# Whole-tile stores and more crossbar transposes in a fused attention and maxout kernel

## The chip, the cores and the metric

One core of one Trainium2 chip. The metric is the device time of one execution, in microseconds (us). Executions of one kernel mostly agree within 0.3%; "fast" and "slow" below are the states that the runs were sorted into, and only fast runs are compared. A profile is one execution taken by the hardware profiler; its span is some 2 us shorter than the time.

Names used in profile lines: PE is TensorE (matmul), PEld its weight loads, DVE VectorE, ACT ScalarE, POOL GpSimd, SP SyncE, which here only issues transfers. L299 is a line of the kernel that was profiled, so line numbers shift between kernels.

## The reference

```python
# attention over pooled keys: B, H, S, D = 8, 8, 576, 64; pool = 8
k_p = k.reshape(B, H, S // 8, 8, D).mean(axis=3)
v_p = v.reshape(B, H, S // 8, 8, D).mean(axis=3)
attn = softmax(q @ k_p.T / sqrt(D))          # 576 x 72 for each batch and head
x = (attn @ v_p).transpose(0, 2, 1, 3).reshape(4608, 512)
# feed-forward with a maximum of three: 512 -> 768 -> 512
h = maximum(maximum(x @ w1, x @ w2), x @ w3)
out = h @ w_out                              # 4608 x 512, float32
```

## The kernel before

The feed-forward runs in nine blocks of 512 tokens. A block is 72 matmuls of 512 columns (hidden) and 24 (project). The attention of the next batch is slipped in between: after each group of matmuls, a "slot", a plan may call some steps. `k` turns the pooled keys, `s0` to `s7` are scores and exponentials by head, `v0` to `v4` the five 128-token chunks of values, `x0` to `x4` their transposes, `T` the transpose of q by the DMA crossbar. TensorE takes all of these in the order of the program, so a step whose input is late stops the feed-forward too (in e4 below, scores whose keys were late stopped it for 1.35 us in each of five blocks).

```python
def turn_x(b, c0, keep, xn, tag, evac=nc.scalar.copy):
    if b > 1:                                 # batches 2 to 7: by the crossbar
        nc.sync.dma_start_transpose(out=xT[:, :, g0 + keep:g0 + 128], in_=...)
        return
    ...                                       # batches 0 and 1: 4 TensorE transposes, one copy

def turn_k(b):
    pkt = keys(b, TR)                         # 6 TensorE transposes into PSUM
    for par in range(2):
        fill_kz(b, par, 0, H, pkt,
                nc.scalar.copy if b == 1 else nc.vector.tensor_copy)
...
# project: one tile is 128 tokens = two row groups (g) of 64 rows, 9 rows apart in HBM
for u in range(2):
    b, g = divmod(2 * m + u, NG)
    dst = out[S * b:S * b + S, :].rearrange("(r g) c -> r g c", g=NG)
    (nc.scalar if last and u else nc.sync).dma_start(
        out=dst[:, GS[g], c], in_=osb[64 * u:64 * u + 64, c])
...
def pool_work(n, mm):                         # called after slot 0 of block n
    if n + 2 < B:
        after([load_k(n + 2)], mm)            # GpSimd's loads for two batches on
        load_q(n + 2)
        load_v(n + 2)
```

The softmax here doesn't subtract the row's maximum and nothing guards it: scores larger than these inputs give would overflow.

## Time and profile before

| | before |
|---|---|
| time, median of the runs beside the changed kernel | 242.82 us |
| span of the profiled execution | 241.0 us |
| TensorE busy | 230.9 us, 96% |
| last matmul ends / span ends | 236.5 / 241.0 us |
| granted TensorE clock, mean | 0.998 |
| a 128 KB store, issue to landing | 2.4 us |

The table is read from the top: TensorE is the bound, and from 50 us on its matmuls start one after another at the pace that their width sets. The prediction below shows the lines.

### The profile page before, as it was taken

To read this page: it belongs to the slowest core of one execution; us is meant where nothing else is said; L and a number is where in the kernel's file an instruction comes from. 1 tells how busy PE (TensorE), PEld (TensorE's weight loads), DVE (VectorE), ACT (ScalarE), POOL (GpSimd) and SP (SyncE) were. 2 spreads that over 40 slices of the span, in tenths; PEclk is the share of its full clock that TensorE was granted. 3 is DMA by queue.
4 is the path that set the end of the run, shared out by engine and by line. 5 is a ranking of instruction groups with operands and counts; after the bars stand their busy time and mean duration, and the time that the engine had idled before them with its cause. 6 is when DMAs were issued, how large, how long until landed. Compare 5 with 4: busy or idle time off the path is not lost.

```text
span 241.0 us, 4221 instructions
## 1 busy us (share of the span) xinstructions
PE 230.9 (96%) x1609; PEld 122.7 (51%) x1609; DVE 131.7 (55%) x239; ACT 100.1 (42%) x173; POOL 123.7 (51%) x91
## 2 busy tenths in 40 slices
PE   7698999999999999999999999999999999999992
PEld 3376555575554555455545554555455544444441
DVE  6856754665583558354836483648364834504530
ACT  2373247546513651365235523552355232142121
POOL 8864276989997479638880979286500000000000
PEclk9999999999999999999999999999999999999999
DMA  7999999999948995699769987997640253043006
GB/s 135 188 198 206 196 202 208 169 166 241 184 97 153 222 166 120 128 194 197 131 125 156 227 176 133 193 192 135 133 93 0 69 123 85 3 108 66 0 20 154
DMA packets 51939, 34.29 MB, mean 142 GB/s; under 512 B 32144, under 2 KB 46480, under 8 KB 51920
## 3 DMA queue, kind: packets, MB, share of 16 engines
q0 software_dynamic: 17088, 17.11, 45.5%
q1 hardware_dynamic: 34672, 16.79, 34.3%
q8 instruction: 12, 0.20, 0.3%
q10 hardware_dynamic: 160, 0.13, 0.2%
q14 instruction: 7, 0.06, 0.1%
HBM read 34.60 MB, written 9.44 MB: 183 GB/s over the span
## 4 chain that ended last, share of the span: by engine, by line
PE 89%; DVE 5%; ACT 2%; DMA 2%; issue 1%; DVEq 0%
PE pw L295 55%; PE po L331 19%; PE psc L203 6%; PE pav L238 4%; DMA kt<-in_k_dram 2%; PE pxt L229 1%; DVE kf L362 1%; ACT et L208 1%; DVE t L304 1%; PE pkt L174 1%; PE pvp L156 1%; DVE xn L246 1%; PE pqt L167 1%; DVE kp L366 1%; DVE kf L364 1%
## 5 line engine op out<-in xcount | busy, mean ns | idle before, releaser
L295 PE MATMUL pw<-xT,mw 128*128 128x512 f16 (+2 forms) x696 | 155.6, 364 | 0.8 <-ACT xT L233 0.7
L295 PEld LDWEIGHTS <-mw 128*128 128x128 f16 x696 | 61.8, 98 | 56.2 <-issue 1.0
L304 DVE TENSOR_TENSOR t<-t,pw 128x512 f16<-128x512 f16 (+2 forms) x58 | 37.8, 651 | 71.0 <-PE pw L295 43.7
L301 ACT CAST t<-pw 128x512 f16<-128x512 f32 (+2 forms) x58 | 32.3, 556 | 56.1 <-PE pw L295 54.8
L331 PE MATMUL po<-mwo,hT 128*128 128x512 f16 (+1 forms) x222 | 50.7, 373 | 0.0
L208 ACT ACTIVATE et<-psc 72x576 f16<-72x576 f32 (+2 forms) x62 | 40.7, 662 | 20.9 <-PE psc L203 20.7
L307 DVE TENSOR_TENSOR hT<-t,pw 128x512 f16<-128x512 f16 (+2 forms) x58 | 37.7, 650 | 9.0 <-PE pw L295 5.3
L336 ACT COPY osb<-po 128x512 f32<-128x512 f32 (+1 forms) x36 | 20.9, 580 | 47.7 <-PE po L331 43.7
L135 POOL TENSOR_TENSOR half<-vt 72x2048 f32<-72x2048 f16 x7 | 28.4, 4060 | 10.0 <-DMA vt<-in_v_dram 9.9
L331 PEld LDWEIGHTS <-hT 128*128 128x128 f16 x222 | 20.3, 97 | 21.3 <-DVE hT L307 2.4
L135 POOL TENSOR_TENSOR half<-kt 96x1536 f32<-96x1536 f16 x6 | 18.5, 3085 | 23.4 <-DMA kt<-in_k_dram 23.3
L246 DVE TENSOR_TENSOR xn<-pav,rcp 128x512 f16<-128x512 f32 x39 | 27.0, 691 | 1.5 <-DVE rcp L244 0.2
L136 POOL TENSOR_TENSOR half<-half 72x1024 f32<-72x1024 f32 (+1 forms) x13 | 27.2, 2096 | 1.0
L203 PE MATMUL psc<-qT,kz 128*128 128x64 bf16 (+3 forms) x192 | 25.9, 246 | 0.4 <-DVE kz L179 0.3
L203 PEld LDWEIGHTS <-kz 128*128 128x128 bf16 x192 | 17.8, 98 | 15.7 <-DVE kz L179 1.5
L238 PEld LDWEIGHTS <-et 72*128 72x128 f16 x312 | 15.2, 98 | 7.6
L238 PE MATMUL pav<-vp,et 72*128 72x65 f16 x312 | 16.5, 194 | 0.0
L244 DVE RECIPROCAL rcp<-pav 128x8 f32<-128x8 f32 x39 | 7.9, 204 | 9.4 <-PE pav L238 9.3
L139 POOL TENSOR_TENSOR kp<-half 96x384 bf16<-96x384 f32 x12 | 11.7, 993 | 0.5
L179 DVE COPY kz<-pkt 64x576 bf16<-64x576 bf16 (+1 forms) x14 | 9.9, 711 | 2.9 <-PE pkt L174 2.7
L79 POOL DMA_DIRECT2D vt<-in_v_dram x10 | 8.0, 804 | 2.9 <-DMA qb<-in_q_dram 2.2
L139 POOL TENSOR_TENSOR vp<-half 72x512 f16<-72x512 f32 x7 | 8.9, 1268 | 0.5
(48 smaller groups left out, 79.1 us busy)
## 6 DMA issues: line engine op xcount, KB each, us to landing
out_dram<-osb SPq DMA_DIRECT2D x70, 128.0 KB, 2.4
kt<-in_k_dram POOLq DMA_DIRECT2D x7, 576.0 KB, 7.4
qb<-in_q_dram POOLq DMA_DIRECT2D x7, 576.0 KB, 12.2
vt<-in_v_dram POOLq DMA_DIRECT2D x7, 576.0 KB, 15.0
mw<-in_moe_w_dram POOLq DMA_DIRECT2D x9, 256.0 KB, 9.3
mwo<-in_moe_w_out_dram POOLq DMA_DIRECT2D x1, 768.0 KB, 18.1
qb<-in_q_dram POOLq DMA_DIRECT2D x2, 288.0 KB, 7.0
xT<-xn SPq DMA_TRANSPOSE x30, 2.4
```

The costliest lines, as they stand in the source:

```text
L135: e.tensor_tensor(out=f, in0=t[:, :, 0:4, :], in1=t[:, :, 4:8, :], op=ALU.add)
L136: e.tensor_tensor(out=f[:, :, 0:2, :], in0=f[:, :, 0:2, :], in1=f[:, :, 2:4, :], op=ALU.add)
L203: nc.tensor.matmul(out, kz_all[b % 2][:, f % 2, h, :], qTs[b][:, n + i0:n + i1, 64 * (h % 2):64 * (h % 2) + 64], start=True, stop=True)
L208: nc.scalar.activation(out=out, in_=in_, func=FT.Exp, scale=1.0 / 64.0)
L238: nc.tensor.matmul(pav[:, h // 4, 65 * (h % 4):65 * (h % 4) + 65], ets[b][:, h, c0:c0 + 128], vp_all[:, b, h, :], start=True, stop=True)
L246: nc.vector.tensor_tensor(out=xn, in0=pv[:, :, :, 0:D], in1=rcp.to_broadcast([128, 2, 4, D]), op=ALU.mult)
L295: mm = nc.tensor.matmul(pw, w_sb[wi][:, kc, bass.ts(jc, 128)], xT[:, kc, col], start=(kc == 0), stop=(kc == KCH - 1))
L301: nc.scalar.copy(out=t, in_=pw)
L304: nc.vector.tensor_tensor(out=t1, in0=t, in1=pw, op=ALU.max)
L307: nc.vector.tensor_tensor(out=hT[:, jc, c0:c1], in0=t, in1=pw, op=ALU.max)
L331: nc.tensor.matmul(po, hT[:, jc, bass.ts(mm, 128)], wo_sb[:, jc, c], start=(jc == 0), stop=(jc == JCH - 1))
L336: nc.scalar.copy(out=osb[:, c], in_=po)
```

## The change

Its intent: take transposes off TensorE (keys of batches 3 to 7, x of batch 1), shorten SyncE's queue by storing a tile with one transfer instead of two, and give the new crossbar transfers time by finer groups in blocks 0 and 1 and a later attention of batch 2.

```diff
     def turn_k(b):
-        pkt = keys(b, TR)
+        pkt = keys(b, TR) if b < 3 else kTs[b]
         for par in range(2):
             fill_kz(b, par, 0, H, pkt,
-                    nc.scalar.copy if b == 1 else nc.vector.tensor_copy)
+                    nc.vector.tensor_copy if b == 2 else nc.scalar.copy)
@@ turn_x
-        if b > 1:
+        if b > 0:
@@ do
+            elif name[0] == "Z":
+                kTs[b] = sb2.tile([128, 6, 96], BF16, name="kT", tag="kT")
+                nc.sync.dma_start_transpose(
+                    out=kTs[b], in_=kps[b].rearrange("p i a d -> p (i a d)"))
@@ hidden: half groups
-            parts = [..., (1, 2, 0, 256), (0, 2, 256, NB), (2, JCH, 0, NB)]
+            parts = [..., (1, 3, 0, 256), (0, 3, 256, NB), (3, JCH, 0, NB)]
         elif n == 1:
-            parts = [(0, 1, 0, 256), (0, 1, 256, NB), (1, JCH, 0, NB)]
+            parts = [(0, 2, 0, 256), (0, 2, 256, NB), (2, JCH, 0, NB)]
@@ project: stores
+                e = nc.scalar if last and c.start == 0 else nc.sync
+                b, g = divmod(2 * m, NG)
+                dst = out[S * b:S * b + S, :].rearrange("(r g) c -> g r c", g=NG)
+                if g < NG - 1 and GS[g] < GS[g + 1]:
+                    step = GS[g + 1] - GS[g]
+                    e.dma_start(out=dst[GS[g]:GS[g + 1] + 1:step, :, c],
+                                in_=osb[:, c])
+                    continue
                 for u in range(2):
                     ...                       # else two stores, as before
@@ plans: block 0 with its steps moved to 34 slots (cut); q of batch 2 ("T") after
@@ batch 1's x, at slot 0 of block 1; the others:
-        b, i = n + 1, 3 * (n == 1)
-        got = {0: [], 3: [], 3 + i: [(b, "k")]}
+        b, i = n + 1, 8 * (n == 1)
+        got = {2 + i: [(b, "k")]}
         got.update({5 + i + h: [(b, f"s{h}")] for h in range(H)})
-        got.update({15 + i + c: [(b, f"v{c} x{c}")] for c in range(5)})
+        got.update({14 + i + c: [(b, f"v{c} x{c}")] for c in range(5)})
+        got[17 + i].append((b + 1, "Z"))
```

A tile whose two row groups lie in one batch and ascend is stored whole: 27 of 36 in one transfer, and the last tile by column halves.

## The prediction

> **What bounds the kernel now.** I read the page's busy table first, then its chain of work that ended last, then that chain in order of time, then the timeline of TensorE and of the two queues that issue transfers (SyncE's and GpSimd's), and last the transfers by issue with their time to landing. The page:
>
> ```profile
> PE 230.9 (96%) x1609; PEld 122.7 (51%) x1609; DVE 131.7 (55%) x239; ACT 100.1 (42%) x173; POOL 123.7 (51%) x91
> ...
> PE 89%; DVE 5%; ACT 2%; DMA 2%; issue 1%; DVEq 0%
> ```
>
> TensorE is busy 96% and carries 89% of the chain. Busy alone proves little, because matmuls overlap; the chain in order of time (start, us, matmuls) settles it:
>
> ```profile
> 195.07 15.54 PE pw L295 x72
> 210.61 5.18 PE po L331 x24
> ```
>
> A block without attention is 96 matmuls of 512 columns in 20.72 us, 0.216 us each with no gap. From the trace's matmul starts I summed what each start-to-start step has beyond the usual one for its width: 9.5 us in all, of which 5.7 before 20 us, 2.0 in 20 to 30, 0.8 in 30 to 50, and under 1.1 in the whole rest. The seven blocks after the first therefore run at TensorE's own pace: only fewer or narrower matmuls can help there. Waits can be won only in block 0 (17 to 48.7 us), and block 1 begins at 48.7, block 2 at 73.4. Block 0 waits like this:
>
> ```profile
> 22.69 1.03 PE L295 MATMUL pw<-xT,mw 128*128 128x256 f16 x8 [0.67 <-ACT xT L233]
> ```
>
> The last part is the transfers around the start of block 1 (SyncE's queue, then GpSimd's, then landings of those in 49.8 to 53.8 us):
>
> ```profile
> 45.21 4.59 SPq L270 DMA_TRANSPOSE qT<-qb  x1
> 49.85 4.43 SPq L340 DMA_DIRECT2D out_dram<-osb  x6
> ```
>
> ```profile
> 46.62 1.95 POOL L139 TENSOR_TENSOR kp<-half 96x384 bf16<-96x384 f32 x2
> 49.59 0.57 POOL L72 DMA_DIRECT2D kt<-in_k_dram  x1 [1.02 <-PE pxt L229]
> 50.15 0.78 POOL L86 DMA_DIRECT2D qb<-in_q_dram  x1
> 50.93 0.85 POOL L79 DMA_DIRECT2D vt<-in_v_dram  x1
> ```
>
> ```profile
> out_dram<-osb SPq DMA_DIRECT2D x6, 128.0 KB, 7.4
> kt<-in_k_dram POOLq DMA_DIRECT2D x1, 576.0 KB, 6.7
> qb<-in_q_dram POOLq DMA_DIRECT2D x1, 576.0 KB, 11.3
> vt<-in_v_dram POOLq DMA_DIRECT2D x1, 576.0 KB, 14.3
> qT<-qb SPq DMA_TRANSPOSE x1, 6.6
> ```
>
> The reader is to see that batch 2's q transpose is issued at 45.2, ahead of the k, q and v loads of batch 3 at 49.6, and lands 6.6 us later, at 51.8; the six stores issued just after those loads took 7.4 us each, against a median of 2.4 over the kernel.
>
> **What the Trainium skill says.** "Perfetto Trace Analysis", Identifying the Most-Contended Engine: matmul busy share is a poor measure because matmuls are pipelined; the trace agrees (a 512-column matmul is listed at 379 ns but starts come every 216), so I count start-to-start time. "DMA: Bandwidth & Descriptors", Queues, rings and completion order: each DMA engine takes turns between queues packet by packet. The trace agrees: in 112 to 113 us, a q transpose beside a v load, 125 transpose packets went beside 150 load packets, and after the load's end 897 to 1030 per us went. The same page, Rules for kernel authors, prefers one 128-partition transfer to two of half the partitions; no run here shows it yet. "TensorE: Matmul & The Clock Gate", Part 1: an idle window of about 3.4 us halves the array's clock, and a busy one restores it. The trace agrees at its end: the granted clock falls to 0.5 some 3 us after the last matmul.
>
> **The change part by part.**
>
> Keys by the crossbar, batches 3 to 7: removes 5 x 6 transposes of 96 columns. Six take 0.42 us with the last one's 0.205 pipeline time, so (0.42 - 0.205)/5 = 0.043 us a step; 30 x 0.042 (the median of starts) = 1.26 us off the path. The evictions (two of 0.64 us a batch) move from VectorE to ScalarE, both about half idle, so nothing. The transfer comes eight or so slots ahead of its use, so it is hidden.
>
> Batch 1's x by the crossbar: 20 transposes of 128 columns at 0.056 us = 1.12 us off the path, and five ScalarE copies gone.
>
> Six half groups in blocks 0 and 1: 12 matmuls of 512 become 24 of 256 in each; 24 x 0.109 - 12 x 0.216 = 0.02 us each. Nothing by itself, but it gives 1.3 us more work on the first 256 columns, while x2 and x3 are being turned. Walking the new slots by hand with the old durations: the waits around x2, x3 and x4 (0.04, 0.32, 0.84 and 0.46 us) nearly vanish (0.2 left); the wait for the key sum (0.31) grows to 0.5 because the slots between are half as long, one of 0.45 appears between the key pooling and the key transposes, and the q turns keep 0.5 of 0.39; the score waits (0.08 and 0.24) shrink to 0.13. So 2.7 becomes about 1.8, 0.9 us better. Block 1 could begin at 48.7 - 0.9 - 12 x 0.056 (its other eight x transposes lay inside block 1) = 47.1 us.
>
> Whole-tile stores: most pairs of 0.54 + 0.59 us on SyncE's queue become one, I assume about 0.6. TensorE does not wait for them, but SyncE's queue gets shorter, and the tail (last matmul start 236.5, end 241.0) has one store fewer behind the last copy: 0.4 us.
>
> Sum without new waits: 1.26 + 1.12 + 0.9 + 0.4 = 3.7; 242.86 - 3.7 = 239.2 us.
>
> **What the change puts in its place.** The order of the changed kernel shows SyncE's queue at the end of block 0 as x0, store, x1, store, x2, two stores, x3, store, x4, then batch 2's q transpose, which block 0 used to issue much earlier. x0's values are made after the last hidden group, at about 42.5 us. An x transpose takes SyncE 1.31 us from issue to issue, a store 0.6: x1 at 44.5, x2 at 46.4, x3 at 49.0, q at 52.2. TensorE's first block 1 matmul waits for x0 and x1, its seventh slot for x2 and x3, and the first score of batch 2 for q.
>
> x1 shares the engines with batch 2's v load, which runs to about 48 (stores issued at 43.9 and 44.5 took 5.6 and 5.2 us). So x1 lands at about 49.6, and block 1 begins 2.5 us late. The k load of batch 3 waits for the end of slot 0 and for GpSimd (free at 48.6), so it is issued at about 50, again ahead of the q transpose. That transpose then waits for k (6.7 us), and shares packet by packet with q and v: those loads have some 1090 packets, at 150 a us 7.3 us, so till about 64; of the transpose's 2304 packets 110 to 190 a us go meanwhile, and the rest takes 1.3 us more. Landing at about 66. Without waits the first score would stand at 47.1 + 12 x 0.436 + 2 x 0.863 + 0.25 = 54.3. So TensorE waits 66 - 54.3 = 11.7 us in block 1, the 2.5 at its start included; and a wait so long halves the clock for some 3.4 us after it, 1.7 us more. Sum: 239.2 + 11.7 + 1.7 = 252.6 us.
>
> **The rivals.**
>
> First, no collision: the later attention (first score at slot 13 in place of 8) and the half groups are just what one would do to give x and q their time, which speaks for somebody having measured it. Then 239 to 240. Against it: all five later q transposes that overlapped a v load landed only 2 us or more after it.
>
> Second, a partial one: q gets its turn as soon as k is through, at about 56, and runs nearly alone: landing 58.5, a wait of 4.2 in all and perhaps no clock loss: 243.5. Against it are the 125 packets a us beside 150.
>
> Third, the collision above: 249 to 253, the lower end if x1 comes early and the loads with it.
>
> A fourth, that a new engine bounds (ScalarE with the key evictions), I rule out: it is busy 42%, and gets 10 x 0.64 us more and five copies less. Stores are off the path whatever they cost.
>
> **Range and chances.** I give the collision 0.58, the partial one 0.15, none 0.27. Only the collision is over 2% slower (over 247.7); no case reaches 2% faster (238.0) unless my block 0 walk is too dark, 0.04. The middle of this is about 249.0 us, range 239.3 to 253.5.
>
> **What would show it.** Right: in block 1 a long TensorE idle before the first scores of batch 2, put down to the q transpose, with a time to landing of over 10 us; a shorter one before the block's first matmul, put down to the x transpose; the granted clock down around 65 us; later blocks 0.25 us shorter each. Wrong: that transpose landing under 7 us, or the k load issued after it; then the time is near 239. A wait before x2 or x3 (slot 6 of block 1) would show that x3 fell behind the k load too.

## The result, and the profile after

The changed kernel took 351.5 us in the median (350.15 to 353.32, four runs), the kernel before 242.82. The ratio is 1.447 (95% interval 1.438 to 1.456). Here and below a ratio is the mean time of one kernel's fast runs over that of the other's of the same rounds, so it isn't quite the ratio of the medians quoted. The prediction was 249.0, with a range to 253.5: right in direction, and far too small.

The page of the changed kernel, its busy row, the slices of granted clock, and the chain that ended last:

```profile
PE 246.7 (71%) x1583; PEld 128.0 (37%) x1583; DVE 123.3 (35%) x232; ACT 110.2 (32%) x181; POOL 123.5 (35%) x91
PEclk9899995686998558999978995799658999999955
PE 59%; DMA 18%; SPq 10%; issue 2%; DVE 2%; ACT 2%; POOL 0%; DVEq 0%; POOLq 0%
```

Read against the lines before: TensorE's share of the chain fell from 89% to 59%, and transfers (DMA 18%) and SyncE's queue (SPq 10%) stand in the chain. TensorE now idles, and its clock is down in many slices. Whom TensorE waits for, in the view of waits (us in total, times, longest):

```profile
PE pw L299 <- DMA xT<-xn: 23.5, 4, 10.4
PE psc L203 <- ACT kz L179: 20.6, 2, 19.9
PE pw L299 <- DMA qT<-qb: 14.0, 1, 14.0
PE pw L299 <- issue: 10.7, 1, 10.7
PE psc L203 <- DMA qT<-qb: 6.1, 1, 6.1
```

Three of the five are waits for crossbar transfers. The copy kz waited in its turn (28.2 us, by the groups of instructions) for the keys' crossbar transfer, and the wait put down to "issue" ends, in the chain in order of time, behind an x transpose (from 213.83 us, 2.54 long). The chain in order of time shows how long single transfers took, where 2.3 to 8 us were usual before:

```profile
55.01 5.14 DMA xT<-xn
60.15 21.72 DMA qT<-qb
...
102.92 23.21 DMA kT<-kp
```

The prediction had the q transpose at about 14 us. The plain loads suffered too. From the transfers by issue, before and then after (KB each, median us to landing; the page of the changed kernel gives no landing time for its stores):

```profile
out_dram<-osb SPq DMA_DIRECT2D x70, 128.0 KB, 2.4
kt<-in_k_dram POOLq DMA_DIRECT2D x7, 576.0 KB, 7.4
```

```profile
out_dram<-osb SPq DMA_DIRECT2D x27, 256.0 KB
kt<-in_k_dram POOLq DMA_DIRECT2D x7, 576.0 KB, 15.1
```

A k load takes twice as long, though nothing about it was changed, and HBM traffic is the same 34.6 MB read and 9.4 written. The last matmuls, where no transpose and no load is left, show the stores alone. The end of the chain before and after:

```profile
231.33 5.21 PE po L331 x30
```

```profile
322.44 5.21 PE po L335 x30
```

Before, the span ends at 241.0, 4.5 us after the end of the last matmul (236.5); after, at 349.3, 21.7 us after it (327.6). Twenty-two microseconds of nothing but stores: what do the DMA engines do then? The stretch 330 to 340 us of the changed kernel (columns: stretch, length, five engines, granted clock, DMA share, GB/s):

```profile
330.00:340.00 10.00, 0.00 (x0) 0.00 (x0) 0.00 (x0) 0.00 (x0) 0.00 (x0) 0.60 0.13 50
```

The share of the 16 engines that is busy is 0.13, that is 2.1 of 16, at 50 GB/s. The trace's 2 KB packets say the same: 84 ns each, 25 in a microsecond, so two at a time. The Trainium skill has the rule, in "DMA: Bandwidth & Descriptors", Why a DMA increments its semaphore by 16 and not by 1: the number of engines is the largest up to 16 that divides the slowest dimension (of size other than 1) of both sides' patterns. The source's is 128 partitions, the destination's 2, so 2. Its Rules for kernel authors warn of just this ("Use all 16 engines"). At 50 GB/s a 256 KB store takes over 5 us (an estimate). How that holds up other transfers shows between 56.5 and 58.5 us, when an x transpose issued at 55.01 had not landed (it did at 60.15):

```profile
DMA packets 50, 0.10 MB, mean 51 GB/s; under 512 B 0, under 2 KB 0, under 8 KB 50
```

All 50 packets that start in these two microseconds are of 2 KB, the stores' own. None of the transpose's, which are smaller, starts.

The loss can be booked from the matmul starts. After 46 us, steps that are over 0.25 us longer than their width asks for sum to 77.8 us (before: none); the smaller excesses, nearly all of them the 427 instead of 216 ns of a 512-column matmul at half clock, to 15.7 us (before 1.0). The tail is 17.2 us longer. That is 77.8 + 14.7 + 17.2 = 109.7, less 2.4 for the transposes removed: 107.3 of the spans' difference of 108.3 us.

### The profile page after: what moved, and what is told of

It reads as the page before. It is cut to its first block, busy times and chain, and to the rows that moved or that the text cites. A ratio compares the mean times of both kernels' runs of the same rounds, so it can differ in the third digit from the quotient of the medians.

```text
span 349.3 us, 4173 instructions
## 1 busy us (share of the span) xinstructions
PE 246.7 (71%) x1583; PEld 128.0 (37%) x1583; DVE 123.3 (35%) x232; ACT 110.2 (32%) x181; POOL 123.5 (35%) x91
## 4 chain that ended last, share of the span: by engine, by line
PE 59%; DMA 18%; SPq 10%; issue 2%; DVE 2%; ACT 2%; POOL 0%; DVEq 0%; POOLq 0%
PE pw L299 36%; PE po L335 13%; DMA kT<-kp 7%; DMA qT<-qb 6%; SPq L270 6%; PE psc L203 5%; SPq L223 3%; DMA xT<-xn 3%; PE pav L238 3%; DMA qb<-in_q_dram 2%; ACT kz L179 1%; PE pqt L167 1%; PE pvp L156 1%; PE wm L363 0%; POOL kt L72 0%
## 5 line engine op out<-in xcount | busy, mean ns | idle before, releaser
L299 PE MATMUL pw<-xT,mw 128*128 128x512 f16 (+2 forms) x720 | 169.4, 381 | 49.0 <-DMA xT<-xn 23.5
L299 PEld LDWEIGHTS <-mw 128*128 128x128 f16 x720 | 67.9, 103 | 112.8 <-issue 31.5
L203 PE MATMUL psc<-qT,kz 128*128 128x64 bf16 (+3 forms) x192 | 28.1, 259 | 27.0 <-ACT kz L179 20.6
L340 ACT COPY osb<-po 128x512 f32<-128x512 f32 (+1 forms) x36 | 20.9, 580 | 56.5 <-PE po L335 44.6
L203 PEld LDWEIGHTS <-kz 128*128 128x128 bf16 x192 | 18.6, 102 | 45.2 <-ACT kz L179 22.1
L135 POOL TENSOR_TENSOR half<-vt 72x2048 f32<-72x2048 f16 x7 | 28.4, 4054 | 17.3 <-DMA vt<-in_v_dram 17.2
L179 ACT COPY kz<-kT 64x576 bf16<-64x576 bf16 x10 | 11.7, 1166 | 28.3 <-DMA kT<-kp 28.2
L72 POOL DMA_DIRECT2D kt<-in_k_dram x9 | 5.1, 565 | 31.0 <-PE pw L299 29.4
L139 POOL TENSOR_TENSOR kp<-half 96x384 bf16<-96x384 f32 x12 | 11.7, 992 | 0.5
## 6 DMA issues: line engine op xcount, KB each, us to landing
kt<-in_k_dram POOLq DMA_DIRECT2D x7, 576.0 KB, 15.1
```

The source lines that it names most:

```text
L135: e.tensor_tensor(out=f, in0=t[:, :, 0:4, :], in1=t[:, :, 4:8, :], op=ALU.add)
L203: nc.tensor.matmul(out, kz_all[b % 2][:, f % 2, h, :], qTs[b][:, n + i0:n + i1, 64 * (h % 2):64 * (h % 2) + 64], start=True, stop=True)
L299: mm = nc.tensor.matmul(pw, w_sb[wi][:, kc, bass.ts(jc, 128)], xT[:, kc, col], start=(kc == 0), stop=(kc == KCH - 1))
```

## The experiments

My theory A: the pattern of the whole-tile stores. Rival B: the crossbar collisions that I had predicted, only worse. Rival C: a large store is slow in itself. Rival D: the key transposes come late for the scores. Every kernel computes the whole result, and all twelve runs were correct.

| run | what | time, us (range) | before beside it |
|---|---|---|---|
| e1_split | changed, stores as before | 269.3 fast; 273.9 to 274.7 slow | 242.88 |
| e2_merge_only | before, whole-tile stores | 314.91 (313.03 to 315.3) | 242.88 |
| e3_interleaved | changed, stores of 64 x 2 rows | 264.73 (263.94 to 264.85) | 242.88 |
| e4_keys_only | before, keys by crossbar | 248.44 (248.06 to 250.35) | 242.88 |
| e5_keys_dve | e4, VectorE fills | 241.75 (241.53 to 242.63) | 242.79 |
| e6_keys_early | e4, one slot earlier | 241.82 (241.6 to 244.22) | 242.79 |
| e7_loads_later | e3, loads of batch 3 later | 248.84 (248.18 to 250.24) | 242.79 |
| e8_stores_interleaved_on_before | before, stores of 64 x 2 rows | 242.51 (242.37 to 243.0) | 242.79 |
| e9_combined | the parts that paid | 240.46 (239.98 to 242.31) | 243.11 |
| e10_x4_too | e9 and one x transpose | 240.15 (239.91 to 241.85) | 243.11 |
| e11_halves_2x32 | before, two stores of 2 x 32 rows | 371.55 (370.29 to 372.24) | 242.87 |
| e12_halves_4x16 | before, two stores of 4 x 16 rows | 304.29 (303.78 to 304.9) | 242.87 |

### e1_split and e2_merge_only: the stores undone, and the stores alone

```diff
 # e1, on the changed kernel; e2 is the reverse, on the kernel before
-                e = nc.scalar if last and c.start == 0 else nc.sync
-                ...                           # one whole-tile store where it fits
                 for u in range(2):
                     b, g = divmod(2 * m + u, NG)
                     dst = out[S * b:S * b + S, :].rearrange("(r g) c -> r g c", g=NG)
                     (nc.scalar if last and u else nc.sync).dma_start(
                         out=dst[:, GS[g], c], in_=osb[64 * u:64 * u + 64, c])
```

> The changed kernel with its stores as they were before: two of 64 rows for each tile in place of one whole-tile store; all else of the change kept. Theory A (the whole-tile stores, whose destination pattern is 2 x 64 rows, move on 2 of the 16 DMA engines only, and everything behind them waits): the time falls from 351.5 to 239 to 255 us, and no transfer of SyncE's queue takes over 15 us. Rival B (the crossbar transposes collide with the loads, as predicted blind): A's part is small, and it stays over 300 us. If A holds, what is left over 239 is the blind prediction's collision of batch 2's q transpose: 249 to 253 if that was right.

> The kernel before with nothing changed but its stores: whole tiles in one transfer, as in the changed kernel. Theory A: over 280 us, with waits before blocks' first matmuls put down to x transposes and q transposes. Rival B: 242 to 243 us, since no crossbar transfer is added.

e2: 314.91 us, ratio 1.294 (1.290 to 1.298), where it adds no crossbar transfer at all. Rival B can't do that. Its longest waits are for the x transposes that the kernel before already had and that never held it up (2.7 us more are for a q transpose):

```profile
PE pw L295 <- DMA xT<-xn: 40.4, 5, 12.7
```

Booked from the matmul starts like the changed kernel, e2's 72 us are some 45 of waits, 10 of lower clock and 17 of tail.

e1: one run was fast, at 269.3; the others and the profile were slow, so I take from it only that some 80 us went with the stores' pattern, and that 269 is above the 255 I had allowed. Something else was left over; e3, all of whose runs were fast, shows it better.

### e3_interleaved: the same stores, another order of rows

The maximum that writes a hidden tile puts the rows of the two groups side by side (partition 2r + u instead of 64u + r), so a store walks 64 x 2 rows instead of 2 x 64.

```diff
-                nc.vector.tensor_tensor(out=hT[:, jc, c0:c1], in0=t, in1=pw, op=ALU.max)
+                ...out=hT[:, jc, c0:c1].rearrange("p (m r u) -> p m u r", r=64, u=2), ...
-                dst = out[S * b:S * b + S, :].rearrange("(r g) c -> g r c", g=NG)
+                dst = out[S * b:S * b + S, :].rearrange("(r g) c -> r g c", g=NG)
-                    e.dma_start(out=dst[GS[g]:GS[g + 1] + 1:step, :, c], ...)
+                    e.dma_start(out=dst[:, GS[g]:GS[g + 1] + 1:step, c], ...)
```

> The changed kernel with the whole-tile stores kept (same bytes, same 2 KB rows, as many transfers), but the two halves' rows interleaved over the partitions, so that the destination pattern is 64 x 2 rows instead of 2 x 64. Theory A (the slowest dimension, 2, sets the number of engines): as e1, within 2 us, and a store lands in some 3 us. Rival C (a store of 256 KB or of 128 partitions is slow in itself): stays over 300 us.

264.73 us. Same bytes, same row length, same number of transfers, and 87 us less than the changed kernel: rival C falls. It is not within 2 us of e1, as I had expected, but 4.6 below e1's one fast run. The stores of 256 KB now land in 2.7 us. What is left over 242.9 is what the prediction was about. The waits of e3:

```profile
PE psc L203 <- DMA qT<-qb: 7.5, 1, 7.5
PE pw L299 <- DMA xT<-xn: 4.7, 2, 3.9
PE psc L203 <- ACT kz L179: 4.3, 2, 3.6
```

and SyncE's queue and GpSimd's at the start of block 1:

```profile
44.54 1.74 SPq L223 DMA_TRANSPOSE xT<-xn  x1
...
52.94 15.58 SPq L270 DMA_TRANSPOSE qT<-qb  x2
```

```profile
52.63 0.56 POOL L72 DMA_DIRECT2D kt<-in_k_dram  x1 [3.01 <-PE pw L299]
```

The k load is issued at 52.6, the q transpose just behind it at 52.9, and that transpose lands 15.7 us later, at 68.6 (issues by time, median us to landing):

```profile
qT<-qb SPq DMA_TRANSPOSE x1, 15.7
```

### e7_loads_later: were the loads what q waited for?

```diff
-                if slot == 0 and n > 0:
+                if slot == (12 if n == 1 else 0) and n > 0:
                     pool_work(n, mms[-1])
```

> As e3_interleaved, with one thing changed: GpSimd's loads of batch 3 (and its folds) are issued after slot 12 of block 1 instead of slot 0, so that batch 2's q transpose has the DMA engines to itself. If those loads are what the q transpose waited for (the blind prediction's step): it lands in 6 to 7 us instead of 15.7, TensorE's wait before batch 2's first score falls from 7.7 to under 1.5 us, the half-clock stretch after it goes too, and the time falls from 264.7 to about 253. If the q transpose was slow for another reason: 264 again. The wait before block 1 (4.1 us, for x) stays in both.

248.84 us, ratio 1.023 (1.016 to 1.029) to the kernel before, 15.9 less than e3. The q transpose of batch 2 landed in 3.9 us:

```profile
qT<-qb SPq DMA_TRANSPOSE x1, 3.9
```

TensorE's wait for it is gone, and the half-clock stretches shrank from 23.9 us in all to 3.4. So the loads were the cause. I had expected 253, above the measured time, mainly because I undervalued the clock: what matmuls lose to it fell by some 5 us, and the waits of block 2 by some 2. The waits for x at the starts of blocks 1 and 2 remain (3.0 and 2.4 us), as expected for the first; the second is for batch 2's x.

### e4, e5, e6: the keys by themselves

```diff
 # e4: on the kernel before, turn_k and "Z" as in the change, the plan otherwise as before
 # e5: also
-                    nc.vector.tensor_copy if b == 2 else nc.scalar.copy)
+                    nc.scalar.copy if b == 1 else nc.vector.tensor_copy)
 # e6: e4 with the fill one slot earlier for n >= 2
-        got = {0: [], 3: [], 3 + i: [(b, "k")]}
+        got = {0: [], 3: []}
+        got.setdefault(3 + i if n == 1 else 2, []).append((b, "k"))
```

> The kernel before with only the keys of batches 3 to 7 by the crossbar. By the blind prediction's sum: 1.26 us less, 241.6 us, same waits. Rival D (the key transposes or their evictions from SBUF, which took 1.17 us each in the changed kernel against the 0.64 predicted, delay the scores): 242.8 or more, with TensorE waiting for kz in each of five blocks.

> The kernel before with the keys of batches 3 to 7 by the crossbar, as in e4_keys_only, but filled in by VectorE from SBUF instead of by ScalarE. Theory: e4's loss is the ScalarE fill alone (two of 1.16 us in place of two short ones, 1.35 us of waiting in each of 5 blocks, 6.75 us against 1.26 us of transposes saved). Then this has no wait before the scores and takes 241.6 us. Rival: the key transfer itself is late; then the same waits stay and it takes about 248.

> As e4_keys_only, the fill still by ScalarE, but in blocks 2 to 6 given one slot earlier (slot 2, as the changed kernel has it). Theory: a slot is 0.86 us and the wait was 1.35, but the fill then goes ahead of the next group's copy in ScalarE's order, so all or most of the waits go: 241.6 to 243 us. Rival: key transfer late: 248.

e4: 248.44 us, a loss where the prediction's sum says 1.26 us gained. The groups of instructions show why, first of the kernel before (ScalarE's two are of batch 1), then of e4, then of e5:

```profile
L179 DVE COPY kz<-pkt 64x576 bf16<-64x576 bf16 (+1 forms) x14 | 9.9, 711 | 2.9 <-PE pkt L174 2.7
L179 ACT COPY kz<-pkt 64x576 bf16<-64x576 bf16 x2 | 1.3, 633 | 0.9 <-PE pkt L174 0.9
```

```profile
L179 ACT COPY kz<-kT 64x576 bf16<-64x576 bf16 x10 | 11.6, 1163 | 0.2
```

```profile
L179 DVE COPY kz<-kT 64x576 bf16<-64x576 bf16 x10 | 6.5, 646 | 0.2
```

ScalarE needs 1163 ns for a fill from SBUF, against 633 for the same shape from PSUM in batch 1; VectorE needs 646 from SBUF. Two fills behind a copy of the hidden group end 1.35 us (0.31 + 1.04) after the scores want them, five times: 6.75 us, and 242.9 - 1.26 + 6.75 = 248.4. With VectorE (e5) the wait is gone, 241.75, ratio 0.994 (0.988 to 0.999), and one slot earlier (e6) it is gone too, 241.82, ratio 0.995 (0.990 to 1.001), which by itself is not clear of noise (one wait of 0.6 us, at a block's start, stays). So the key transfer was never late here, and the change had e6's cure in it: in the changed kernel k stands at slot 2. In the changed kernel the keys do come late (20.6 us of waits, above), but with the stores mended 4.3 are left (e3): there it is mostly the stores that delay them. D by itself explains e4 and little of the 351 us.

### e8: whole-tile stores on 16 engines, on the kernel before

The edit is e3's, on the kernel before.

> The kernel before with nothing but interleaved whole-tile stores (as in e3, 16 engines). Theory: stores are off the path; only the tail gains 0.3 to 0.5 us: 242.5. Rival (a whole-tile store costs in itself): over 244.

242.51 us, ratio 0.996 (0.991 to 1.001): the tail's gain at best, and not clear of noise. Against e2, the same kernel with stores of the same size and number, it is 72 us less: that pair is the plainest test of the pattern.

### e11, e12: half-size stores with a bad pattern

Nothing is merged here; each of the two stores of 64 rows walks its rows as q x (64/q) with q = 2 or 4.

```diff
+                    dst = out[S * b:S * b + S, :].rearrange(
+                        "(a q g) c -> g q a c", g=NG, q=2)      # e12: q=4
+                    ...dma_start(out=dst[GS[g], :, :, c], in_=osb[64 * u:64 * u + 64, c])
```

> The kernel before with its two 64-row stores for each tile kept, nothing merged, but the rows of each half permuted over the partitions so that the destination pattern is 2 x 32 rows instead of 64. If the slowest dimension of the pattern sets how many DMA engines carry a store (2 here), this is as bad as the whole-tile stores of e2_merge_only, 300 to 330 us, though no store is larger than before. If the size of a store or its 128 partitions was the trouble: 242 to 245.

> The same with 4 x 16 rows: 4 engines, half as long on each. Between the two: each of the 4 engines then carries 8 x 1.35 = 11 us of stores in a block of 24 us instead of 21.5, so loads and transposes wait much less: 245 to 270 us. At 242 to 243 the number of engines would matter only when it is 2; at 300 and more it would not be the number of engines at all.

371.55 and 304.29 us. Both are misses (300 to 330 and 245 to 270 were expected), and a time over 300 for e12 was to speak against the number of engines. But the times are not clean: the permuted write of the hidden tile (steps of 64 and 32 bytes) also takes VectorE 2.4 and 2.3 us instead of 0.7, and TensorE waits for it in both, by the waits 16.4 and 15.1 us for the hidden tile and 14.1 and 13.3 for the values that stand behind it on VectorE. The longest waits of e12:

```profile
PE pw L295 <- DVE hT L307: 15.1, 30, 0.7
PE po L334 <- DVE rcp L244: 13.3, 7, 2.0
```

After block 0 none of e12's waits is for a transfer: its loss is VectorE's, the clock's, and a tail of 12.8 us in place of 4.5. So e12's time does not measure what 4 engines cost. In e11 TensorE waits 31.1 us for x transposes and 11.9 for q transposes besides, and the tail is 22.6 us. VectorE's cost is much the same in both (218 and 213 us busy), so most of the 67 us between them are the engines' doing. The stretches with only stores in flight are clean, e11 first, then e12:

```profile
352.00:360.00 8.00, 0.00 (x0) 0.00 (x0) 0.00 (x0) 0.00 (x0) 0.00 (x0) 0.50 0.13 48
```

```profile
294.00:300.00 6.00, 0.00 (x0) 0.00 (x0) 0.00 (x0) 0.00 (x0) 0.00 (x0) 0.50 0.26 94
```

A slowest dimension of 2 gives a share of 0.13 (2 of 16) and 48 GB/s, of 4 a share of 0.26 (4 of 16) and 94 GB/s, with stores of half the size of the change's. Counted from the start and end of each packet, two are in flight for nine tenths of the stretch shown of the changed kernel and of e11's, four for three quarters of e12's, and 16 or more for half of e3's last 8 us. The pattern sets it.

### e9, e10: the parts that paid, together

e9 is the kernel before with e5's keys, e8's stores and block 0 with six half groups; batch 1's x stays on TensorE and q of batch 2 stays where it was.

```diff
-            parts = [..., (1, 2, 0, 256), (0, 2, 256, NB), (2, JCH, 0, NB)]
+            parts = [..., (1, 3, 0, 256), (0, 3, 256, NB), (3, JCH, 0, NB)]
-              13: [(1, "a")], 15: [(1, "K")], 17: [(1, "k")], 19: [(1, "Q0")], ...
+              15: [(0, "x4"), (1, "a")], 18: [(1, "K")], 21: [(1, "k")], 22: [(1, "Q0")], ...
 # e10: also
-        if b > 1:
+        if b > 1 or (b == 1 and keep):
```

> What the earlier runs left standing, on the kernel before: keys of batches 3 to 7 by the crossbar with VectorE's fill (e5), whole-tile stores interleaved (e8), and block 0 with six half groups and its steps moved to suit, batch 1's x and q as before. By the sums: 242.8 - 1.26 - 0.35 - about 0.9 for block 0's waits = 240.3 us. If block 0's waits only move, as the 0.50 and 0.44 us waits of the changed kernel suggest, 241.2.

> As e9_combined, and only the last part of batch 1's x (x4, which no matmul needs before block 2) by the crossbar: 4 transposes of 0.056 us less, 0.2 us, and no wait, since it has a whole block to land: 240.1 us. Rival (any crossbar transfer at that time costs a wait): above e9_combined.

240.46 us, ratio 0.991 (0.987 to 0.995), and 240.15, ratio 0.989 (0.985 to 0.993). Both beat both kernels, by about 1%. The chain of e9 is TensorE's again, at 89%.

That e10 is better than e9 isn't shown by ranges that overlap; that it isn't worse in the median agrees with the expectation.

## Why the prediction was wrong

**The step that failed** is "Stores are off the path whatever they cost", with its "I assume about 0.6" for a merged store and its gain of 0.4 us. Only the issue on SyncE's queue was judged. That part was right at first (0.5 to 0.7 us each up to 119 us in the changed kernel; its last four took 12.8 us together). What was not looked at is the pattern: 2 x 64 rows on 2 of 16 engines. The term was -0.4 us; e3 against the changed kernel puts it at 87 us. The prediction quoted the skill's rule that prefers one 128-partition transfer, noted that no run showed it, and passed over the rule on the number of engines on the same page. (A small misreading beside it: 236.5 us is where the last matmul ends, not where it starts; no sum of the prediction rests on it.) And a store off TensorE's path is not off the path of the transposes that share its engines: e2 shows that, with 40.4 us of waits for x.

**The collision in block 1** was right in mechanism and nearly in size, as e3 shows once the stores are mended. x1 was issued at 44.54 (predicted 44.5), q at 52.9 (52.2), behind the k load; q landed at 68.6 (66); TensorE waited 4.1 us before block 1 (2.5) and 7.7 before the first score (the rest of the 11.7 predicted): 11.8 in all, by the matmul starts (the view of waits shows 3.9 and 7.5). That the sum fits so well is part luck: q landed 2.6 us later than predicted, and the lower clock had put off the matmuls that come before the first score by as much. e7 took the loads away, and the wait went. The second rival (q has its turn when k is through) and the first (no collision) both fall.

**Two terms were too small.** The clock: 1.7 us were put down for one dip. e3 has 23.9 us at half clock, in three stretches that each begin in a long wait, and the small excesses of its matmul steps sum to 8.1 us against 1.0. And the same collision a block later was not foreseen: block 2's keys, x and scores cost 6.1 us more of waits in e3. 252.6 (the prediction's sum for the collision) plus 5.4 for the clock and 6.1 is 264.1, against 264.7 measured.

**The keys**: 1.26 us off the path, right as far as the noise lets one see (e5: 1.04 us less in the medians). "So nothing" for moving the fill to ScalarE was wrong in size, 1.16 us a fill and not 0.64, and harmless at slot 2 only.

**Block 0**: new waits of 0.50 and 0.44 us were predicted as 0.5 and 0.45, and the block's last step ended at 47.2 in e3 (47.1). From its first hidden matmul to that step the block took 30.3 us, against 31.7 up to block 1 in the kernel before; 0.7 of the difference are the x transposes removed, so some 0.7 are left of the 0.9 predicted. In e9 the same stretch took 31.4 us, only 0.3 less than before: of the 2.8 us between the profiled spans, 0.4 lie before block 0, which e9 does not change, 1.2 in blocks 2 to 7 (the keys), and 0.9 in the last block with its tail. That e9 met its 240.3, with 0.9 for block 0 in the sum, is in part luck.

**Batch 1's x by the crossbar** was to save 1.12 us; in e7 the wait for it before block 1, 3.0 us, cost more than that, so only its last part, x4, was kept in e10.

## What to carry to other kernels

Before two transfers are joined into one, write down both sides' patterns and look at the outermost dimension: the join that makes the partition side nicer can put a 2 outermost on the HBM side, and then two DMA engines carry it and everything else on those engines waits. Reordering the rows so that the large dimension is outermost cost little here: 729 ns in place of 687 for VectorE's write of a hidden tile, and no time that shows (e8). A transfer that nobody waits for is still in the way of those that somebody waits for, so the DMA share in a stretch with only that transfer (0.13 here) is worth a look before its issue cost is.

## What the Trainium skill lacked or had wrong

- "DMA: Bandwidth & Descriptors", Rules for kernel authors: the row on two transfers to disjoint partition halves says to use one 128-partition transfer. Here the join cost 72 us on the kernel before (e2) and 87 in the changed kernel (e3) with a destination of 2 x 64 rows, and gained at most 0.3 us (e8) with 64 x 2. The row should point to the one on all 16 engines, whose example is a broadcast; a strided HBM side that puts 2 outermost is as easy to write. The rule on the number of engines itself is right: shares of 0.13 and 0.26 of 16 for 2 and 4.
- No page gives a figure for how the time of ScalarE's copy depends on its source: 64 x 576 bf16 with a strided read took 1163 ns from SBUF and 633 from PSUM, while VectorE took 646 from SBUF. "ScalarE: Activation LUTs" says that ScalarE is closer to PSUM and VectorE to SBUF, but its advice is on destinations. No run here has an unstrided read, so what is the memory's part and what the stride's stays open.
- "SBUF — State Buffer", the note on 16-byte lines, gives no cost for a write that changes lines at each element: a VectorE write with steps of 32 to 64 bytes took 2.3 to 2.4 us for 128 x 512 fp16, against 0.73 with steps of 4 bytes. The measured rates for strided streams in "Vector Engine (DVE) Microarchitecture Reference" are of 4-byte elements only.
